# Two of three token groups go through w_in with seven block products in place of eight

## The chip, the cores and the metric

The kernel runs on one core of a Trainium2 chip. The metric is the device time of one execution in microseconds (us). Engines are named as in the profile: PE is TensorE's matmul, PEld its weight load, DVE is VectorE, ACT is ScalarE, POOL is GpSimd, and SP issues the DMAs.

## What is computed

Windowed attention over 2 batches, 8 heads and 768 positions gives 1536 tokens of width 512; two feed-forward layers follow, each with a first matrix `w_in` (512 x 2048), a pointwise function, and a second matrix `w_out` (2048 x 512).

```python
def _moe_ref(x, w_in, w_out):                 # layer 1 (L = 0 in the code)
    h = x @ w_in
    g = h * (1.0 / (1.0 + np.exp(-h)))
    return (g @ w_out).astype(np.float32)

def _moe2_ref(x, w_in, w_out):                # layer 2 (L = 1)
    h = x @ w_in
    g = np.maximum(0.01 * h, h)
    return (g @ w_out).astype(np.float32)

def reference(**kwargs):
    ...
    x = np.ascontiguousarray(attn_out.transpose(0, 2, 1, 3)).reshape(B * S, H * D)
    x = _moe_ref(x=x, **moe_kwargs)
    return _moe2_ref(x=x, **moe2_kwargs)
```

## The kernel before

The 1536 tokens are three groups of 512 (`gi` = 0, 1, 2). Each layer's 2048 inner columns are 16 chunks of 128, four to a part, so a layer has four parts. Activations lie transposed, 128 features by 512 tokens, in four tiles `x` (layer 1) or `xn` (layer 2), one for each 128 of the 512 features (`kk`). The weights come as 64-bit numbers; `load` turns a chunk into float32 with one ScalarE instruction and three VectorE instructions (L260 to L269). Every matmul operand, weight or activation, is then split into a high part (a rounded copy, index 0) and a low part (the rest, index 1): the copy is done by ScalarE or VectorE (L219, L221), the rest by a VectorE subtraction (L275). A product of two such operands takes three matmuls (`PASSES`: high by high, low by high, high by low), so a "triplet" of 512-column matmuls is the smallest piece of work on PE here.

`unit_in` makes one chunk of `h` for one group: 4 triplets into one PSUM bank `ph` (L305), then ScalarE (L313 or L315), VectorE (L320 or L322), ScalarE (L325) and VectorE (L328) make the split tile `g`. `unit_out` makes one 128-row slice of the product with `w_out` over the four chunks of a part: 4 triplets into a bank `po` (L358); ScalarE stores it in `y` in the first part (L372), VectorE adds it to `y` in the later ones (L390). After layer 1 the sums are split into `xn` (L404, L407). One group in one part thus costs 16 triplets at L305 and 16 at L358.

No order of instructions is written down by hand. `Sched` holds every piece of work as a task with a duration, a priority, its dependencies and the buffers it needs, plays them through on PE, DVE, ACT and SP with numbers of buffers from `SIZES` (8 PSUM banks `ps`, 6 tiles `g`, 5 chunks of `wi`, 6 of `wo`, 3 staging buffers `st`, ...), and writes the instructions out in the order in which they started there. Each engine then runs its own list in that order. Attention and the first part of layer 1 are interleaved in this way.

## Time and profile before

| | us |
|---|---|
| median of 3 runs | 630.77 (630.51 to 631.47) |
| the profiled execution's own time | 630.69 |
| its span, first to last instruction | 628.9 |
| PE busy in the span | 616.7 |
| DVE busy | 432.8 |
| ACT busy | 275.8 |

The profile is of one execution, so sums are made against its own 630.69 us; it lies 0.08 us under the median. Between the span and the time lie 1.79 us that the trace does not cover. In the first 143 us PE alternates between attention and the feed-forward; from there to the end it does nothing but triplets. Busy time of PE is not a measure of its work, since matmuls overlap in the records (a record lasts some 0.39 us, while one starts every 0.2267 us); its idle time is.

### The profile page before, as it was taken

The numbers are of one execution on the slowest core, as the hardware profiler recorded it, in microseconds if no ns is written. First come the engines' busy times: TensorE is split into PE (matmuls) and PEld (weight loads), VectorE is DVE, ScalarE is ACT, GpSimd is POOL, SyncE is SP. The second block draws the span as 40 slices with busy tenths as digits, with TensorE's granted clock in tenths as the row PEclk, the third lists the DMA queues.
The fourth block names the chain that finished last, engine by engine and source line by source line (L and its number), as shares of the span: only waits on it lengthen the run. The fifth ranks groups of instructions, "written<-read, shape, count | busy, mean of one in ns | idle before, by whom it ended". The sixth has DMA issues, their size and how long they took to land.

```text
span 628.9 us, 8667 instructions
## 1 busy us (share of the span) xinstructions
PE 616.7 (98%) x3191; PEld 501.1 (80%) x3191; DVE 432.8 (69%) x993; ACT 275.8 (44%) x612; POOL 2.2 (0%) x18
## 2 busy tenths in 40 slices
PE   7999999999999999999999999999999999999996
PEld 4687777778888888888888888888888888888885
DVE  6999889889653967396748881776369745954333
ACT  5898878855541244124434453444233233213210
POOL 1000000000000000000000000000000000000000
PEclk8999999999999999999999999999999999999999
DMA  8976445213230323023302330133004110200112
GB/s 189 234 181 165 114 97 141 58 40 128 68 100 1 101 69 100 1 77 91 101 1 65 103 90 11 55 113 95 6 16 132 57 64 1 68 0 18 50 68 72
DMA packets 72673, 49.40 MB, mean 79 GB/s; under 512 B 50480, under 2 KB 67120, under 8 KB 72624
## 3 DMA queue, kind: packets, MB, share of 16 engines
q1 hardware_dynamic: 72336, 48.77, 28.0%
q8 instruction: 27, 0.44, 0.3%
q14 instruction: 22, 0.18, 0.1%
q10 hardware_dynamic: 288, 0.00, 0.0%
HBM read 45.62 MB, written 3.15 MB: 78 GB/s over the span
## 4 chain that ended last, share of the span: by engine, by line
PE 92%; DVE 6%; DMA 1%; issue 0%; ACTq 0%; DVEq 0%; ACT 0%
PE po L358 42%; PE ph L305 41%; PE s L618 3%; PE pa L670 3%; PE pv L690 3%; DVE A L630 1%; PE pt L576 1%; DVE A L653 1%; DVE f L266 1%; DMA nraw<-in_n_local_dram 1%; DVE f L269 0%; DVE wi L275 0%; DVE x L699 0%; DVE f L263 0%; DVE rs L644 0%
## 5 line engine op out<-in xcount | busy, mean ns | idle before, releaser
L305 PE MATMUL ph<-x,wi 128*128 128x512 f32 (+1 forms) x624 | 146.0, 379 | 1.2 <-DVE x L699 0.4
L358 PE MATMUL po<-g,wo 128*128 128x512 f32 x576 | 139.8, 392 | 0.0
L305 PE MATMUL ph<-xn,wi 128*128 128x512 f32 x576 | 136.9, 389 | 0.0
L358 PE MATMUL po<-wo,g 128*128 128x512 f32 (+1 forms) x588 | 136.4, 385 | 0.0
L305 PEld LDWEIGHTS ph<-x,wi 128*128 128x128 f32 x624 | 110.7, 188 | 24.7 <-issue 2.2
L358 PEld LDWEIGHTS po<-wo,g 128*128 128x128 f32 x588 | 108.9, 188 | 22.0
L305 PEld LDWEIGHTS ph<-xn,wi 128*128 128x128 f32 x576 | 108.1, 188 | 22.4
L358 PEld LDWEIGHTS po<-g,wo 128*128 128x128 f32 x576 | 107.1, 188 | 23.1 <-issue 1.3
L328 DVE TENSOR_TENSOR g<-t,g 128x512 fp32r<-128x512 f32 (+1 forms) x100 | 66.6, 669 | 41.5 <-ACT g L325 40.1
L325 ACT ACTIVATE g<-t 128x512 fp32r<-128x512 f32 (+1 forms) x100 | 61.2, 616 | 66.2 <-DVE t L322 37.8
L315 ACT ACTIVATE t<-ph 128x512 f32<-128x512 f32 x48 | 28.6, 596 | 91.4 <-PE ph L305 90.5
L322 DVE TENSOR_TENSOR t<-t,ph 128x512 f32<-128x512 f32 x48 | 32.9, 686 | 37.6 <-ACT t L315 37.6
L260 ACT ACTIVATE st<-st 128x512 f32<-128x512 f32 x64 | 43.0, 672 | 31.9 <-DMA st<-in_moe_w_out_dram 23.7
L390 DVE SCALAR_TENSOR_TENSOR yp<-po,yp 128x512 f32<-128x512 f32 x48 | 33.1, 689 | 32.2 <-PE po L358 32.2
L313 ACT ACTIVATE t<-ph 128x512 f32<-128x512 f32 (+1 forms) x52 | 29.2, 563 | 53.9 <-PE ph L305 53.2
L637 ACT ACTIVATE A<-A,nm 128x256 f32<-128x256 f32 (+1 forms) x96 | 46.3, 486 | 6.0 <-DVE nm L630 5.6
L266 DVE SCALAR_TENSOR_TENSOR f<-st,f 128x512 int32<-128x512 int32 x64 | 44.0, 690 | 1.2
L269 DVE SCALAR_TENSOR_TENSOR f<-st,f 128x512 int32<-128x512 int32 x64 | 43.9, 687 | 0.5
L320 DVE SCALAR_TENSOR_TENSOR t<-t,ph 128x512 f32<-128x512 f32 (+1 forms) x52 | 33.1, 644 | 15.1 <-ACT t L313 15.0
L630 DVE CUSTOM_DVE_ANT_0 A<-s,mask 128x256 f32<-128x256 f32 (+1 forms) x96 | 35.2, 396 | 6.8 <-PE s L618 6.7
L670 PE MATMUL pa<-ident,A 128*128 128x128 f32 x176 | 26.4, 279 | 3.6 <-DVE A L653 2.4
L390 DVE SCALAR_TENSOR_TENSOR yo<-po,yp 128x512 f32<-128x512 f32 (+1 forms) x25 | 16.7, 669 | 18.9 <-PE po L358 18.9
(67 smaller groups left out, 431.4 us busy)
## 6 DMA issues: line engine op xcount, KB each, us to landing
st<-in_moe_w_in_dram SPq DMA_DIRECT2D x32, 512.0 KB, 3.7
st<-in_moe_w_out_dram SPq DMA_DIRECT2D x32, 512.0 KB, 3.5
vd<-in_v_dram SPq DMA_DIRECT2D x24, 128.0 KB, 3.0
q<-in_q_dram SPq DMA_DIRECT2D x22, 128.0 KB, 3.0
k<-in_k_dram SPq DMA_DIRECT2D x22, 128.0 KB, 3.0
out_dram<-yo SPq DMA_DIRECT2D x11, 256.0 KB, 2.0
vp<-in_v_dram SPq DMA_DIRECT2D x20, 96.0 KB, 2.7
vp<-in_v_dram SPq DMA_DIRECT2D x20, 32.0 KB, 2.4
```

Of the source, the lines that this page charges most:

```text
L260: eng.activation(hf, hf, AF.Copy, scale=2.0 ** -112)
L266: eng.scalar_tensor_tensor(fi(), lo(), 29, fi(), op0=ALU.logical_shift_right, op1=ALU.bitwise_or)
L269: eng.scalar_tensor_tensor(fi(), hi(), -(2 ** 31), fi(), op0=ALU.bitwise_and, op1=ALU.bitwise_or)
L305: eng.matmul(ph()[:, :w], wv[:, a, kk, :], xs[kk]()[:, b, cs], start=(kk == 0 and i == 0), stop=(kk == NKK - 1 and i == 2),)
L320: eng.scalar_tensor_tensor(tt, tt, 1.0, ph()[:, :w], op0=ALU.add, op1=ALU.mult)
L325: eng.activation(g()[:, 0, cs], t()[:, :w], AF.Copy)
L328: eng.tensor_tensor(g()[:, 1, cs], t()[:, :w], g()[:, 0, cs].bitcast(F32), op=ALU.subtract)
L358: eng.matmul(po()[:, :w], lhsT, rhs, start=(j == 0 and i == 0), stop=(j == FPP - 1 and i == 2))
L390: eng.scalar_tensor_tensor(dst()[:, cs], po()[:, :w], scale, y()[:, cs], op0=ALU.mult, op1=ALU.add)
L630: eng.tensor_tensor_reduce(A()[:, i, j, c0:256], s[j]()[:, i, c0:256], mask0 if c0 else mask, -QSCALE * SLOPE[2 * hp + j], 3.0e38, ALU.add ...
L637: eng.activation(a, a, AF.Exp, bias=nm()[:, x:x + 1], scale=-1.0, accum_out=su()[:, x:x + 1])
L670: eng.transpose(pa()[:, j, c, :], A()[:, i, j, c * P:(c + 1) * P], ident)
```

## The change

For groups 0 and 1, and two neighbouring chunks of `w_in` (a pair), the product is written as a product of two 2 x 2 block matrices. The weights' blocks are A11, A12 (the first chunk, lower and upper 256 of the 512 features) and A21, A22 (the second chunk); the activations' blocks are B of the lower and upper features by group 0 and group 1. A block product is two triplets (a block of weights covers two of the four 128-feature tiles). The plain product takes eight of them, 16 triplets for a pair of chunks and two groups. The change takes seven (a Strassen-Winograd scheme), 14 triplets, and adds sums:

- sums of weight blocks, S1 to S4, made by `combine` for each pair behind the weights' conversion (four half-width subtractions or additions, two splits into tiles `ws`);
- sums of activation blocks, T1 to T4, made by `sums` once in a layer (tiles `xs`; in layer 1 the split activations are first added up again);
- sums of products, made by `unit_quad`: bank a is copied to SBUF by ScalarE, five VectorE additions combine it with the banks b, c and d, and three of the four banks take a second product on top of a first one that has been read meanwhile.

`nonlin` then does what L313 to L328 did, for three of four results from SBUF and not from PSUM; in layer 2 these three need no ScalarE instruction ahead. Group 2 keeps `unit_in`, and part one of layer 1, which runs beside attention, is as before. The order in which work is offered to the planner is new: the two quads of a part, then the output of group 0, the input of group 2, the outputs of groups 1 and 2. `wi` has 4 buffers and no longer 5, `wo` 5 and no longer 6; the new tiles lie in a pool `late` that takes the place of the attention's pools, so that nothing of it can be written before the last attention unit has ended (`attn`).

The core of the diff (in layer 1, `first` is part two; in layer 2, part one):

```diff
-            w = Buf(tag, lambda: self.wp.tile([P, 2, DM], F32R, tag=tag, name=tag, bufs={"wi": 5, "wo": 6}[tag]))
...
+            w = Buf(tag, lambda: self.wp.tile([P, 2, DM], F32R, tag=tag, name=tag, bufs=SIZES[tag]))
...
+            self.f[fc % 2] = (f, t)
+            if which == "in" and self.isquad(L, fc // FPP) and fc % 2:
+                self.combine(L, fc // 2, prio)
+        def combine(self, L, pair, prio):
+            add = self.sc.add
+            (fa, _), (fb, t) = self.f[0], self.f[1]
+            res = []
+            H = DM // 2
+            for x in range(2):
+                sf = Buf("sf", lambda: self.late().tile([P, DM], F32, tag="sf", name="sf", bufs=SIZES["sf"]))
+                ws = Buf("ws", lambda: self.late().tile([P, 2, DM], F32R, tag="ws", name="ws", bufs=SIZES["ws"]))
+                if x == 0:
+                    s1 = sf
+                    ops = [(sf, 0, fb, 0, fb, 1, ALU.add), (sf, 1, sf, 0, fa, 0, ALU.subtract)]
+                else:
+                    ops = [(sf, 0, fa, 0, fb, 0, ALU.subtract), (sf, 1, fa, 1, s1, 1, ALU.subtract)]
+                for (o, oh, p, ph, q_, qh, op) in ops:
+                    def fn(eng, o=o, oh=oh, p=p, ph=ph, q_=q_, qh=qh, op=op):
+                        half = lambda b, h: b()[:, h * H:(h + 1) * H]
+                        eng.tensor_tensor(half(o, oh), half(p, ph), half(q_, qh), op=op)
+                    t = add("DVE", 0.36, fn, prio, (t, *self.attn), tuple({id(b): b for b in (o, p, q_)}.values()))
...
+                h = add(AD, (0.52, 0.36), hi, prio, (t, *self.attn), (sf, ws))
+                res.append((ws, add("DVE", 0.62, lo, prio, (h,), (sf, ws))))
+            self.w["sum", L, pair] = res
...
+        def sums(self, L):
+            add = self.sc.add
+            self.T = [[None] * 2 for _ in range(5)]
+            for kk in range(2):
+                B = {}
+                for r in range(2):
+                    for c in range(2):
+                        e = 2 * r + kk
+                        if L == 1:
+                            B[r, c] = (self.y[c, e], self.ydone[c, e])
+                            continue
+                        x = self.xs[0][c][e]
+                        f = Buf("tl", lambda: self.late().tile([P, TG], F32, tag="tl", name="tf", bufs=SIZES["tl"]))
+                        def whole(eng, x=x, f=f):
+                            eng.tensor_tensor(f(), x()[:, 0, :].bitcast(F32), x()[:, 1, :].bitcast(F32), op=ALU.add)
+                        deps = [q[2] for q in self.xdone[0][c][e]]
+                        B[r, c] = (f, add("DVE", 0.62, whole, -0.5, (*deps, *self.attn), (x, f)))
+                def make(i, p, q_, o):
...
+                    hl = [] if L == 0 or i == 3 else [self.xdone[1][{1: 0, 2: 1, 4: 0}[i]][{1: 0, 2: 2, 4: 2}[i] + kk][0][2]]
...
+                    t = add("DVE", 0.62, sub, -0.5, (pt_, qt_, ft, *hl), tuple({id(b): b for b in (f, pb, qb)}.values()))
+                    h = add("ACT", 0.52, hi, -0.5, (t, *self.attn), (f, x))
+                    self.T[i][kk] = (x, add("DVE", 0.62, lo, -0.5, (h,), (f, x)))
+                    return (f, t)
+                t1 = make(1, B[0, 1], B[0, 0], B[0, 0])
+                t3 = make(3, B[1, 1], B[0, 1], (B[0, 1][0], t1[1]))
+                t2 = make(2, B[1, 1], t1, (B[1, 1][0], t3[1]))
+                make(4, B[1, 0], t2, B[1, 0])
...
+        def unit_quad(self, n0, n1, L, pair):
...
+            j0 = (2 * pair) % FPP
+            wa, wb = self.w["in", L, 2 * pair], self.w["in", L, 2 * pair + 1]
+            (s12, t12), (s34, t34) = self.w["sum", L, pair]
+            A11, A12, A22 = (wa, 0), (wa, 1), (wb, 1)
+            S1, S2, S3, S4 = ((s12, t12), 0), ((s12, t12), 1), ((s34, t34), 0), ((s34, t34), 1)
+            X = lambda gi, r: [(self.xs[L][gi][2 * r + kk], self.xdone[L][gi][2 * r + kk][-1][2]) for kk in range(2)]
+            T = self.T
+            bank = {c: Buf("ps", lambda: self.ps.tile([P, TG], F32, tag="ps", name="pq")) for c in "abcd"}
+            def prod(c, A, Bx, first, deps=()):
+                (wt_, wd), half = A
+                def fn(kk):
+                    def mm(eng):
+                        wv = wt_().rearrange("p a (c f) -> p a c f", c=NKK)
+                        for i, (a, b) in enumerate(PASSES):
+                            eng.matmul(
+                                bank[c]()[:, :], wv[:, a, 2 * half + kk, :], Bx[kk][0]()[:, b, :],
+                                start=(first and kk == 0 and i == 0), stop=(kk == 1 and i == 2),
+                                skip_group_check=not first,
+                            )
+                    return mm
+                m = None
+                for kk in range(2):
+                    m = add("PE", 3 * 0.2267, fn(kk), self.pos, (wd, m, Bx[kk][1], *deps), (wt_, bank[c], Bx[kk][0]))
+                self.pos += 0.01
+                return m
+            tl = lambda: Buf("tl", lambda: self.late().tile([P, TG], F32, tag="tl", name="tq", bufs=SIZES["tl"]))
+            def dve(fn, deps, bufs):
+                return add("DVE", 0.62, fn, -1.0, deps, bufs)
+            p1 = prod("a", A11, X(0, 0), True)
+            p6 = prod("b", S2, T[2], True)
+            p5 = prod("c", S1, T[1], True)
+            p7 = prod("d", S3, T[3], True)
+            u2, u4, c12 = tl(), tl(), tl()
+            ba, bb, bc, bd = (bank[c] for c in "abcd")
+            e1 = add("ACT", 0.55, lambda eng: eng.activation(u2(), ba(), AF.Copy), -1.0, (p1, *self.attn), (ba, u2))
+            tu2 = dve(lambda eng: eng.tensor_tensor(u2(), u2(), bb(), op=ALU.add), (e1, p6), (u2, bb))
+            tu4 = dve(lambda eng: eng.tensor_tensor(u4(), u2(), bc(), op=ALU.add), (tu2, p5), (u2, u4, bc))
+            c22 = dve(lambda eng: eng.tensor_tensor(u4(), u4(), bd(), op=ALU.add), (tu4, p7), (u4, bd))
+            p2 = prod("a", A12, X(0, 1), False, (e1,))
+            p3 = prod("c", S4, X(1, 1), False, (tu4,))
+            p4 = prod("d", A22, T[4], False, (c22,))
+            t12_ = dve(lambda eng: eng.tensor_tensor(c12(), u2(), bc(), op=ALU.add), (tu2, p3), (u2, c12, bc))
+            t21_ = dve(lambda eng: eng.tensor_tensor(u2(), u2(), bd(), op=ALU.add), (t12_, p4), (u2, bd))
+            for (nn, j, src, dep) in ((n0, j0, ba, p2), (n1, j0 + 1, u4, c22), (n1, j0, c12, t12_), (n0, j0 + 1, u2, t21_)):
+                self.nonlin(nn, j, src, dep, src is ba, L)
...
+        def nonlin(self, n, j, src, dep, psum, L):
+            add = self.sc.add
+            g, gt = self.gbuf(n, j)
+            if L == 0 or psum:
+                t = Buf("t", lambda: self.tp.tile([P, TG], F32, tag="t", name="t"))
+                bufs = (src, t)
+                def act(eng):
+                    if L == 0:
+                        eng.activation(t(), src(), AF.Tanh, scale=0.5)
+                    else:
+                        eng.activation(t(), src(), AF.Copy, scale=0.01)
+                dep = add("ACT", 0.55, act, -1.0, (dep,), bufs)
+            else:
+                t, bufs = src, (src,)
...
+            c = add("DVE", 0.62, comb, -1.0, (dep,), bufs)
+            h = add("ACT", 0.52, hi, -1.0, (c,), (t, g))
+            gt.append(add("DVE", 0.62, lo, -1.0, (h,), (t, g)))
...
+            for n in range(NGR, N if self.quad else 0, NGR):
+                L, part, _ = self.groups[n]
+                if part == self.first[L]:
+                    self.sums(L)
+                for x in range(FPP // 2):
+                    self.unit_quad(n, n + 1, L, part * (FPP // 2) + x)
+                out(n)
+                I(n + 2, range(FPP))
+                out(n + 1)
+                out(n + 2)
+    SIZES = {"st": 3, "f": 2, "wi": 4, "wo": 5, "g": 6, "t": 3, "ps": 8, "qT": 3, "A": 2, "AT": 4, "tl": 4, "gl": 2,
+             "sf": 2, "ws": 2}
     for gi in range(NGR):
         for e in range(4):
             SIZES[f"x{gi}{e}"] = SIZES[f"y{gi}{e}"] = SIZES[f"k{e}"] = 1
+    for i in range(1, 4):
+        for kk in range(2):
+            SIZES[f"T{i}{kk}"] = 1
...
+        ea = es.enter_context(ExitStack())
+        apool = lambda name, bufs=1: ea.enter_context(tc.tile_pool(name=name, bufs=bufs))
+        ld = apool("ld", 2)
+        kp = apool("kT", 1)
+        ap_ = apool("a", 2)
+        sm = apool("sm", 4)
...
-        mo = Moe(sc, (wp, sp, cv, gp, tp, kp, xp, ps), xt, xdone,
-                 lambda L, gi, e: f"k{e}" if gi == NGR - 1 else f"y{gi}{e}")
+        mo = Moe(sc, (wp, sp, cv, gp, tp, yp, xp, ps), xt, xdone, late)
+        mo.attn = tuple(u["end"] for u in units)```

What this does to the order of the instructions is shown at three places. In the lists, a row is one instruction (x3: a triplet), output and inputs are tile names with their numbers, `pq` is a bank of a quad, `ph` and `po` are those of `unit_in` and `unit_out`.

PE, where part two of layer 1 begins. Before, the last rows of part one's output (`po`) and the first `unit_in` of part two that follow them:

```order
L358 MATMUL po_2345<-g_2152,wo_744 128x512 x3
L358 MATMUL po_2332<-g_2257,wo_931 128x512 x3
L358 MATMUL po_2345<-g_2158,wo_863 128x512 x3
L358 MATMUL po_2332<-g_2269,wo_1111 128x512 x3
L358 MATMUL po_2345<-g_2257,wo_931 128x512 x3
L305 MATMUL ph_2372<-x_312,wi_2141 128x512 x3
L358 MATMUL po_2345<-g_2269,wo_1111 128x512 x3
L305 MATMUL ph_2372<-x_400,wi_2141 128x512 x3
```

Now the first quad stands there: `pq_2345` is bank a (product 1), `pq_2364` bank b (product 6), `pq_2371` bank c (product 5, later 3 on top), `pq_2388` bank d (product 7, later 4); `xs` are sums of activations and `ws` sums of weights.

```order
L404 MATMUL pq_2364<-xs_2193,ws_2318 128x512 x3
L404 MATMUL pq_2371<-xs_2176,ws_2318 128x512 x3
L404 MATMUL pq_2364<-xs_2287,ws_2318 128x512 x3
L404 MATMUL pq_2371<-xs_2240,ws_2318 128x512 x3
L404 MATMUL pq_2388<-xs_2183,ws_2335 128x512 x3
L404 MATMUL pq_2345<-x_495,wi_2135 128x512 x3
L404 MATMUL pq_2388<-xs_2253,ws_2335 128x512 x3
L404 MATMUL pq_2345<-x_567,wi_2135 128x512 x3
L404 MATMUL pq_2371<-x_1229,ws_2335 128x512 x3
L404 MATMUL pq_2388<-xs_2206,wi_2164 128x512 x3
```

The products that need sums stand right behind part one's output, and the second products of the banks c and d (the last two rows) follow the first ones with four and two triplets between them.

VectorE, from the end of attention on. Before, the last attention result (`x_1888`) was followed by conversion of weights and by part one's results:

```order
L699 TENSOR_TENSOR x_1888<-pv_2102,x_1888 128x256
L221 CAST wi_2130<-f_2052 128x512
L275 TENSOR_TENSOR wi_2130<-f_2052,wi_2130 128x512
L320 SCALAR_TENSOR_TENSOR t_2132<-t_2132,ph_1972 128x512
L320 SCALAR_TENSOR_TENSOR t_2138<-t_2138,ph_2015 128x512
```

Now the sums of the activations begin there; of them the rows at the head (`tf` is an activation tile added up again, L366 a difference, L372 the low part of its split):

```order
L914 TENSOR_TENSOR x_1889<-pv_2097,x_1889 128x256
L353 TENSOR_TENSOR tf_2121<-x_315 128x512
L353 TENSOR_TENSOR tf_2126<-x_1046 128x512
L353 TENSOR_TENSOR tf_2133<-x_495 128x512
L507 SCALAR_TENSOR_TENSOR t_2131<-t_2131,ph_2019 128x512
L353 TENSOR_TENSOR tf_2146<-x_1229 128x512
L507 SCALAR_TENSOR_TENSOR t_2141<-t_2141,ph_2027 128x512
L515 TENSOR_TENSOR g_2148<-t_2131,g_2148 128x512
L366 TENSOR_TENSOR tf_2121<-tf_2126,tf_2121 128x512
L515 TENSOR_TENSOR g_2161<-t_2141,g_2161 128x512
L366 TENSOR_TENSOR tf_2126<-tf_2146,tf_2126 128x512
L372 TENSOR_TENSOR xs_2176<-tf_2121,xs_2176 128x512
```

The conversion of the weights of part two has moved behind the sums, as far as it was not done before the end of attention.

VectorE, in the first quad of part two of layer 1. Before, a result took two VectorE instructions there, with conversion of weights between them:

```order
L320 SCALAR_TENSOR_TENSOR t_2238<-t_2238,ph_2191 128x512
L266 SCALAR_TENSOR_TENSOR f_2245<-st_2195,f_2245 128x512
L320 SCALAR_TENSOR_TENSOR t_2255<-t_2255,ph_2212 128x512
L328 TENSOR_TENSOR g_2257<-t_2238,g_2257 128x512
L269 SCALAR_TENSOR_TENSOR f_2245<-st_2195,f_2245 128x512
L328 TENSOR_TENSOR g_2269<-t_2255,g_2269 128x512
```

Now (L429 to L435 are the additions of products, L309 the half-width sums of weights for the next pair, L316 the low part of their split):

```order
L429 TENSOR_TENSOR tq_2368<-tq_2368,pq_2364 128x512
L309 TENSOR_TENSOR sf_2392<-f_2337 128x256
L430 TENSOR_TENSOR tq_2394<-tq_2368,pq_2371 128x512
L309 TENSOR_TENSOR sf_2392<-sf_2392,f_2333 128x256
L221 CAST ws_2404<-sf_2392 128x512
L309 TENSOR_TENSOR sf_2406<-f_2333,f_2337 128x256
L431 TENSOR_TENSOR tq_2394<-tq_2394,pq_2388 128x512
L316 TENSOR_TENSOR ws_2404<-sf_2392,ws_2404 128x512
L459 SCALAR_TENSOR_TENSOR t_2415<-t_2415,pq_2345 128x512
L459 SCALAR_TENSOR_TENSOR t_2418<-t_2418,tq_2394 128x512
L309 TENSOR_TENSOR sf_2406<-f_2333,sf_2392 128x256
L435 TENSOR_TENSOR tq_2437<-tq_2368,pq_2371 128x512
```

L430 must have read bank c before product 3 may be added into it, and L431 bank d before product 4; between them in the queue stand sums of weights.

## Rows read from the trace of the kernel before

**Rows 1.** The page, part 1: busy us (share of the span) xinstructions of each engine.
```profile
PE 616.7 (98%) x3191; PEld 501.1 (80%) x3191; DVE 432.8 (69%) x993; ACT 275.8 (44%) x612; POOL 2.2 (0%) x18
```

**Rows 2.** The page, part 4: chain that ended last, by engine.
```profile
PE 92%; DVE 6%; DMA 1%; issue 0%; ACTq 0%; DVEq 0%; ACT 0%
```

**Rows 3.** Windows: us, then busy of PE, PEld, DVE, ACT, POOL; clock; DMA share; GB/s.
```profile
48.00:64.00 16.00, 14.80 (x132) 11.59 (x129) 14.97 (x54) 14.14 (x43) 0.00 (x0) 1.00 0.65 171
...
160.00:176.00 16.00, 16.00 (x72) 13.28 (x71) 10.94 (x19) 6.86 (x13) 0.00 (x0) 1.00 0.37 103
...
208.00:224.00 16.00, 16.00 (x72) 13.24 (x72) 15.39 (x27) 4.25 (x8) 0.00 (x0) 1.00 0.44 131
...
592.00:608.00 16.00, 16.00 (x72) 13.26 (x71) 6.58 (x11) 3.10 (x5) 0.00 (x0) 1.00 0.13 50
```

**Rows 4.** Chain in order of time: start us, us, what; at its end.
```profile
596.71 9.52 PE po L358 x42
607.59 4.08 PE ph L305 x18
613.03 10.37 PE po L358 x57
```

**Rows 5.** Timeline at the attention's end: start us, us, engine, line, operation, tiles.
```profile
139.82 0.39 PE L690 MATMUL pv<-AT,vd 128*64 128x128 f32 x4
...
140.14 1.65 PE L358 MATMUL po<-g,wo 128*128 128x512 f32 x6
...
140.67 0.42 DVE L699 TENSOR_TENSOR x<-pv,x 128x256 fp32r<-128x256 f32 x1 [1.18 <-ACT x L696]
```

**Rows 6.** Groups by shape: busy us, mean ns of one, idle before and its releasers.
```profile
L322 DVE TENSOR_TENSOR t<-t,ph 128x512 f32<-128x512 f32 x48 | 32.9, 686 | 37.6 <-ACT t L315 37.6
...
L263 DVE TENSOR_SCALAR f<-st 128x512 int32<-128x512 int32 x64 | 26.9, 423 | 0.9
...
L275 DVE TENSOR_TENSOR wi<-f,wi 128x512 fp32r<-128x512 f32 x32 | 22.0, 687 | 0.4
...
L221 DVE CAST wi<-f 128x512 fp32r<-128x512 f32 x22 | 9.4, 427 | 7.9 <-PE ph L305 7.4
...
L494 DVE TENSOR_TENSOR mask<-mk 128x256 f32<-128x256 f32 x1 | 0.4, 425 | 0.0
```

**Rows 7.** Groups by shape, ScalarE.
```profile
L325 ACT ACTIVATE g<-t 128x512 fp32r<-128x512 f32 x92 | 58.2, 634 | 66.2 <-DVE t L322 37.8 <-DVE t L320 28.4
...
L315 ACT ACTIVATE t<-ph 128x512 f32<-128x512 f32 x48 | 28.6, 596 | 91.4 <-PE ph L305 90.5
```

**Rows 8.** Timeline of VectorE in two stretches in which it never sits idle.
```profile
271.90 0.68 DVE L320 SCALAR_TENSOR_TENSOR t<-t,ph 128x512 f32<-128x512 f32 x1
272.50 0.68 DVE L275 TENSOR_TENSOR wi<-f,wi 128x512 fp32r<-128x512 f32 x1
...
283.07 0.69 DVE L266 SCALAR_TENSOR_TENSOR f<-st,f 128x512 int32<-128x512 int32 x1
283.80 0.69 DVE L269 SCALAR_TENSOR_TENSOR f<-st,f 128x512 int32<-128x512 int32 x1
...
289.35 0.69 DVE L328 TENSOR_TENSOR g<-t,g 128x512 fp32r<-128x512 f32 x1
...
464.61 0.69 DVE L275 TENSOR_TENSOR wi<-f,wi 128x512 fp32r<-128x512 f32 x1
...
483.80 0.68 DVE L322 TENSOR_TENSOR t<-t,ph 128x512 f32<-128x512 f32 x1
```

**Rows 9.** Timeline of one chunk's result in a quiet stretch, and a matmul's record.
```profile
257.68 0.39 PE L358 MATMUL po<-g,wo 128*128 128x512 f32 x1
...
262.93 0.60 ACT L313 ACTIVATE t<-ph 128x512 f32<-128x512 f32 x1 [11.90 <-PE ph L305]
263.56 0.69 DVE L320 SCALAR_TENSOR_TENSOR t<-t,ph 128x512 f32<-128x512 f32 x1 [3.40 <-ACT t L313]
264.28 0.63 ACT L325 ACTIVATE g<-t 128x512 fp32r<-128x512 f32 x1 [0.76 <-DVE t L320]
```

More of the change, by code (lines that the diff above doesn't have):

```diff
@@ new lines, in isquad, with ypool, gbuf @@
+        def isquad(self, L, part):
+            return self.late is not None and self.first[L] <= part
+        def ypool(self, gi):
+            return self.late() if self.late and gi == NGR - 1 else self.yp
+        def gbuf(self, n, j):
+            if (n, j) not in self.g:
+                if self.isquad(*self.groups[n][:2]) and j == FPP - 1:
+                    b = Buf("gl", lambda: self.late().tile([P, 2, TG], F32R, tag="gl", name="g", bufs=SIZES["gl"]))
+                else:
+                    b = Buf("g", lambda: self.gp.tile([P, 2, TG], F32R, tag="g", name="g"))
+                self.g[n, j] = (b, [])
+            return self.g[n, j]
@@ L295, in unit_in @@
             t = Buf("t", lambda: self.tp.tile([P, TG], F32, tag="t", name="t"))
[L296 to L298 removed]
+            g, gt = self.gbuf(n, j)
             xs = self.xs[L][gi]
@@ L374, in evac @@
                         eng.tensor_scalar(y(), po(), scale, None, op0=ALU.mult)
-                self.ydone[gi, e] = add("ACT", 0.55, evac, -1.0, (m,), (po, y))
+                self.ydone[gi, e] = add("ACT", 0.55, evac, -1.0, (m, *(self.attn if gi == NGR - 1 else ())), (po, y))
                 return
             y = self.y[gi, e]
-            if not last:
+            if not last or (L == 0 and self.quad and gi < 2):
                 dst = y
@@ L392, in acc @@
                 )
-            a = add("DVE", 0.07 + 0.55 * r, acc, -1.0, (m, self.ydone[gi, e]), (po, y, dst))
+            a = add("DVE", 0.07 + 0.55 * r, acc, -1.0, (m, self.ydone[gi, e]), (po, y, dst) if dst is not y else (po, y))
             self.ydone[gi, e] = a
-            if not last:
+            if not last or (L == 0 and self.quad and gi == 1 and e < 2):
                 return
@@ L515 @@
         add("DVE", 0.6, lambda eng: flags(), 20.0, (mtask,), at=20.0)
-        zero = const.tile([P, TG], mybir.dt.bfloat16, name="zero")
+        zero = kp.tile([P, TG], mybir.dt.bfloat16, name="zero")
         nc.vector.memset(zero, 0.0)
```

85 lines of the change are left out of this document (59 added, 26 removed).

## The prediction

> **What bounds the kernel now.** I read the page first, then the chain of waits, then the windows. The page gives PE 98% of the span [rows 1], and the chain that ends last runs through PE for 92% of it [rows 2]. A busy share alone proves little, so the windows decide: until about 64 us PE has gaps (14.80 of 16 us busy at 48 to 64 us), and from there to the end it has none, while VectorE is anywhere between 6.6 and 15.4 of 16 us [rows 3]. The chain in order of time shows the rate: 42 matmuls of 512 columns in 9.52 us, 0.2267 us each, without a gap up to 623.40 us [rows 4]; a triplet is 0.680 us. The granted clock is 1.00, the upper of its two levels (2.4 GHz), in all these windows [rows 3]. So a triplet that is taken away after the attention gives back 0.680 us, as long as PE still never waits. The whole question is whether VectorE and ScalarE can deliver the sums in time.
>
> **What is removed.** A pair of chunks costs 14 triplets and not 16, for groups 0 and 1 together. There are two pairs to a part and seven changed parts (three of layer 1, four of layer 2): 14 x 2 = 28 triplets, 84 matmuls. The order of the changed kernel has 28 triplet rows less on PE, so it does what it says. At 0.2267 us that is 19.04 us, all of it on the path [rows 2, 4]. If nothing waits: 630.69 - 19.04 = 611.65 us. A changed part has 276 matmuls, 62.6 us of PE; before it had 288, 65.3 us.
>
> **What is added, and its prices.** Per pair VectorE gets four half-width sums of weights and two full-width low parts, and five full-width additions of products; per layer it gets 16 full-width instructions for the T sums (24 in layer 1). No such row exists before; the nearest are subtractions of SBUF tiles (687 ns) and a maximum of an SBUF tile with a bank (686 ns) for the full width, one 128x256 sum (425 ns) for the half width [rows 6]. The reading of SBUF or PSUM makes no difference between these rows, so I take 0.69 and 0.425 us as durations, with casts and shifts at 0.43 [rows 6]. Together: 14 x (4 x 0.425 + 7 x 0.69) + 40 x 0.69 = 119 us more on VectorE, 433 to about 552 of then some 612 us.
>
> Durations overstate what a full queue costs. In a stretch where VectorE never idles, an instruction that doesn't need the one before it starts 0.60 us after it (271.90 to 272.50), one that does 0.73 us after it (283.07 to 283.80). Over two whole stretches, 29 instructions (22 long, 7 short; 18.1 us by duration) took 17.45 us, and 33 (24 long, 9 short; 20.3 us) took 19.19 us [rows 8]: 0.96 and 0.94 of the durations. I take 0.94, the lower one, because conversions, in which each instruction needs the one before, are a smaller part of the new order; the ends are 0.60 and 0.36 us for each long and short one, and the bare durations.
>
> The Trainium skill, page "VectorE: DVE Perf Modes", section "The DRAIN you can't avoid", says that the next instruction doesn't start until the pipeline is empty. By that rule the bare durations would hold; the 0.60 us above speak against it for independent instructions, 0.73 us for it where one needs the other. What the time would be by the rule is rival B.
>
> With these, counted from the changed order between the first addition of one part's first quad and that of the next, VectorE has: layer 1 part two 82 long and 27 short, 64.0 us (58.9 to 68.1); part three 60.4 (55.7 to 64.3); part four 57.7; layer 2 part one 79 and 33, 64.4 us (59.3 to 68.5); then 55.3, 54.1 and 32.5. PE has 62.6 us in each. So two parts are full to the brim and the others have room.
>
> ScalarE gets a copy of bank a per pair (0.60 us), the high parts of the T sums (0.63 us), and those of the weight sums that VectorE doesn't take; it loses three copies per pair in layer 2 (0.60 us) [rows 7]. At 276 us busy of 629 [rows 1] it has room for that: nothing on the path.
>
> **Where PE could wait, place by place.**
>
> *Entry.* PE's order is the same as before until shortly ahead of the attention's end; up to there ScalarE and VectorE only lack the conversion of a fifth `wi` chunk. The last attention product ends at 140.2 us, VectorE's last instruction for it at 141.1 [rows 5]; in the new order one triplet less stands ahead of it, so PE is 0.7 us earlier. From there PE has 41 triplets, 27.9 us, to the first product that needs sums: 140.2 - 0.7 + 27.9 = 167.4 us. VectorE has 35 long and 4 short to that point, 24.3 us (22.4 to 25.8): 165.4 (163.5 to 166.9). It fits: 0. The tiles of the new pool also wait for the attention's reads and loads, which are over by then: 0.
>
> *First part with quads.* VectorE keeps a backlog: the conversion of part two's `w_out` stands behind the sums. To the last of its four chunks it has 87 long and 17 short from 141.1 us on, 63.2 us (58.3 to 67.3), so 204.3 (199.4 to 208.4). PE needs that chunk 91 triplets after attention's end, at 201.4 us. The wait is 2.9 us (0 to 7.0). Behind that point VectorE only follows the outputs of PE and wins the room back.
>
> *First part of layer 2.* The T sums of layer 2 stand in the last output of layer 1, the first weights' sums for the second pair and `w_out` behind them. From the first addition to the fourth `w_out` chunk VectorE has 48 long and 10 short, 35.1 us (32.4 to 37.4); PE needs it 50 triplets after product 6, 34.0 us, less 0.2 us for the last matmul's tail (a record of 0.39 us against 0.2267 [rows 9]). The wait is 1.3 us (0 to 3.6).
>
> *Bank handover in each quad.* Product 3 waits for the addition that reads bank c, product 4 for that which reads bank d. After product 6, four triplets and more (2.7 us) cover a tail of 0.16 and two additions with hops of 0.03 us (262.93 + 0.60 to 263.56 [rows 9]), 1.6 us. After product 7 two triplets (1.36 us) cover a tail, a hop and one addition, 0.9 us: 0.46 us to spare, less than one long instruction in front. ScalarE, which copies bank a, waits on PE alone there. I take 0.1 us for each of 14 quads, 1.4 us (0 to 4.2, at 0.3).
>
> *Buffers.* With four `wi` and five `wo` the next weights come later, but the first chunk of the next part is converted 34 triplets, 23 us, before its use in the order, and DMA runs at 0.13 to 0.44 of its time there [rows 3]: 0. If that cover were gone, a load and its conversion would show, some 6 us a part; nothing points to it.
>
> Sum: 611.65 + 2.9 + 1.3 + 1.4 = 617.25 us; low end 611.65, high end 611.65 + 7.0 + 3.6 + 4.2 = 626.5. The profiled run is 0.08 us under the median, which changes nothing. I say 617.3.
>
> **Rivals.**
>
> *A, PE never waits.* For it: before, PE had no gap even where VectorE was 15.39 of 16 us busy [rows 3], and by the 0.60 us pitch every place above comes out at zero. Against: two parts with more than 62.6 us of work at the measured ratio. 611.7 us.
>
> *B, VectorE sets the pace of three parts.* With bare durations layer 1 part two loses 7.0 us, part three 64.3 - 62.6 = 1.7, layer 2 part one 5.9; with the handovers 16.0 us: 627.7 us. Against it stand both ratios below one [rows 8].
>
> *C, slower than before.* The handover becomes a wait in every quad, because VectorE comes to it with a queue in front: the second part's cover is 0.46 us, and a further long instruction ahead of the addition costs 0.60. The gain is gone when each of the 14 quads waits 19.04 / 14 = 1.36 us, that is from three more long instructions on ((3 x 0.60 - 0.46) = 1.34). With four it is 14 x 1.94 = 27.2 us: 638.8 us. For it: VectorE runs in its order and waits itself for ScalarE (37.6 us idle ahead of L322 alone [rows 6]), and what stands behind the waiting instruction waits with it. Against: in the order only half-width sums and a cast stand between the additions, and five of the seven parts have room.
>
> **How the numbers follow.** The forecast's mechanism, waits of 1.5 to 13 us in the two full parts and at handovers (613 to 625 us), gets 0.74, A 0.10, B 0.07, C 0.06, and 0.03 is left for sums that happen to end within 0.2% of before, which is about what a measurement here can tell from no change (1.3 us). Range 611.5 to 626.5 us: it takes in A and the upper bounds of the three waits and leaves out B, C and the rest, 0.16. Faster by over 0.2%: 0.74 + 0.10 + 0.07 = 0.91; same 0.03; slower 0.06.
>
> **What would show it.** PE should have 3107 instructions and idle about 5 us more than 12.2 us; its waits should name VectorE: `wo` or `ws` low parts between about 185 and 205 us and again in the first 35 us of layer 2, and next to nothing in layer 2 parts two to four, where the triplets should run at 0.680 us. VectorE should be near 550 us busy. The changed parts should take 62.6 us but for the two named. I am wrong if PE waits in every quad for L430 or L431 (C), if windows of the two full parts show PE without a gap (A), if part three of layer 1 is stretched too (B), or if the clock falls below 1.00 behind a wait.

## The result and the profile after

The changed kernel takes 612.77 us (611.97 to 613.20) against 631.12 us, a ratio of 0.9708 (0.9691 to 0.9724): 18.4 us less. A second set (run e1 below) gives 0.9705 (0.9692 to 0.9718), 19.1 us less. The 84 triplet matmuls that are gone are worth 19.04 us. The forecast of 617.3 us had 5.6 us of waits in it that did not come: it is rival A, PE never waits, that happened. The time lies in the range only because the range's low end was set to take in A; the mechanism that was given 0.74 did not show.

The profiled execution took 613.08 us (span 611.3). Its page, busy time and chain by engine, against [rows 1, 2]:

```profile
PE 598.4 (98%) x3107; PEld 485.9 (79%) x3107; DVE 519.6 (85%) x1172; ACT 300.4 (49%) x657; POOL 2.2 (0%) x18
...
PE 93%; DVE 5%; DMA 1%; issue 0%; SPq 0%; ACT 0%; ACTq 0%; DVEq 0%
```

PE is idle for 12.9 us (611.3 - 598.4), before for 12.2. VectorE has 87 us more and PE has not noticed. The windows, against [rows 3] (busy of PE, PEld, DVE, ACT, POOL; clock; DMA share; GB/s); the last one is the first part of layer 2:

```profile
160.00:176.00 16.00, 16.00 (x73) 13.24 (x72) 15.71 (x32) 7.77 (x14) 0.00 (x0) 1.00 0.22 67
176.00:192.00 16.00, 16.00 (x72) 13.28 (x71) 15.85 (x28) 10.08 (x18) 0.00 (x0) 1.00 0.11 33
192.00:208.00 16.00, 16.00 (x73) 13.24 (x72) 15.70 (x28) 8.17 (x14) 0.00 (x0) 1.00 0.44 132
354.60:416.50 61.90, 61.90 (x274) 51.26 (x273) 60.03 (x111) 31.10 (x53) 0.00 (x0) 1.00 0.32 97
```

VectorE is full in the stretches that the prediction named (15.7 to 15.9 of 16 us; 60.03 of 61.90), and in others too (15.97 of 16 us from 480 to 496 us, in layer 2's part three). PE shows no gap in the named ones, the sign that the prediction had given for A. The list of what PE's weight loads waited for from 150 us on has one line (us in total, times, longest):

```profile
PEld pq L404 <- DVE tq L431: 0.3, 1, 0.3
```

It is the handover in the first quad of layer 2's part two. PE starts its triplet there 0.07 us late (424.73 us, where 423.98 + 0.68 = 424.66) and the one behind it another 0.11 us:

```profile
423.99 0.68 DVE L431 TENSOR_TENSOR tq<-tq,pq 128x512 f32<-128x512 f32 x1
```

```profile
423.98 0.84 PE L404 MATMUL pq<-xn,ws 128*128 128x512 f32 x3
424.73 0.96 PE L404 MATMUL pq<-xs,wi 128*128 128x512 f32 x3
425.52 0.86 PE L404 MATMUL pq<-xn,ws 128*128 128x512 f32 x3
```

How close it is elsewhere, the timelines tell. Layer 1's part two: the low parts (L278) of its four `w_out` chunks on VectorE, and L431, the addition that frees bank d for product 4, in the second quad:

```profile
141.20 1.89 DVE L353 TENSOR_TENSOR tf<-x 128x512 f32<-128x512 f32 x3
...
185.48 0.69 DVE L431 TENSOR_TENSOR tq<-tq,pq 128x512 f32<-128x512 f32 x1
...
188.57 0.69 DVE L278 TENSOR_TENSOR wo<-f,wo 128x512 fp32r<-128x512 f32 x1
...
194.92 0.68 DVE L278 TENSOR_TENSOR wo<-f,wo 128x512 fp32r<-128x512 f32 x1
...
198.64 0.68 DVE L278 TENSOR_TENSOR wo<-f,wo 128x512 fp32r<-128x512 f32 x1
...
201.05 0.69 DVE L278 TENSOR_TENSOR wo<-f,wo 128x512 fp32r<-128x512 f32 x1
```

and PE there:

```profile
186.64 0.84 PE L404 MATMUL pq<-xs,wi 128*128 128x512 f32 x3
...
189.36 2.88 PE L545 MATMUL po<-g,wo 128*128 128x512 f32 x12
...
196.16 2.88 PE L545 MATMUL po<-g,wo 128*128 128x512 f32 x12
...
199.56 5.60 PE L545 MATMUL po<-g,wo 128*128 128x512 f32 x24
```

Each group of four output triplets needs one more chunk, so the chunks are wanted at 189.36, 196.16, 199.56 and 202.28 us (199.56 + 4 x 0.68); they are ready at 189.26, 195.60, 199.32 and 201.74. The smallest margin is 0.10 us. L431 ends at 186.17, and product 4 wants its bank at 186.64: 0.47 us. In the first part of layer 2 the fourth chunk is ready at 390.61 + 0.68 = 391.29 us and wanted at 385.90 + 8 x 0.68 = 391.34:

```profile
385.90 8.32 PE L545 MATMUL po<-wo,g 128*128 128x512 f32 x36
...
390.61 0.68 DVE L278 TENSOR_TENSOR wo<-f,wo 128x512 fp32r<-128x512 f32 x1
```

### The profile page after: what moved, and what is told of

It reads as the page before. It is cut to its first block, busy times and chain, and to the rows that moved or that the text cites. A ratio compares the mean times of both kernels' runs of the same rounds, so it can differ in the third digit from the quotient of the medians.

```text
span 611.3 us, 8732 instructions
## 1 busy us (share of the span) xinstructions
PE 598.4 (98%) x3107; PEld 485.9 (79%) x3107; DVE 519.6 (85%) x1172; ACT 300.4 (49%) x657; POOL 2.2 (0%) x18
## 4 chain that ended last, share of the span: by engine, by line
PE 93%; DVE 5%; DMA 1%; issue 0%; SPq 0%; ACT 0%; ACTq 0%; DVEq 0%
PE po L545 43%; PE pq L404 22%; PE ph L492 17%; PE s L833 3%; PE pa L885 3%; PE pv L905 3%; PE pt L791 2%; DVE A L845 1%; DVE A L868 1%; DMA nraw<-in_n_local_dram 1%; DVE f L269 0%; DMA k<-in_k_dram 0%; DVE wi L278 0%; DVE f L266 0%; DVE f L272 0%
## 5 line engine op out<-in xcount | busy, mean ns | idle before, releaser
L545 PE MATMUL po<-g,wo 128*128 128x512 f32 x576 | 139.0, 391 | 0.0
L545 PE MATMUL po<-wo,g 128*128 128x512 f32 (+1 forms) x588 | 135.6, 385 | 0.0
L545 PEld LDWEIGHTS po<-wo,g 128*128 128x128 f32 x588 | 108.9, 188 | 22.0
L545 PEld LDWEIGHTS po<-g,wo 128*128 128x128 f32 x576 | 107.2, 188 | 22.9 <-issue 1.0
L492 PE MATMUL ph<-x,wi 128*128 128x512 f32 (+1 forms) x336 | 78.0, 369 | 1.1 <-ACT x L911 0.4
L492 PEld LDWEIGHTS ph<-x,wi 128*128 128x128 f32 x336 | 56.6, 188 | 13.5 <-issue 2.2
L404 PE MATMUL pq<-xs,ws 128*128 128x512 f32 x252 | 63.8, 389 | 0.0
L263 ACT ACTIVATE st<-st 128x512 f32<-128x512 f32 x64 | 42.9, 670 | 27.4 <-DMA st<-in_moe_w_out_dram 19.4
L404 PEld LDWEIGHTS pq<-xs,ws 128*128 128x128 f32 x252 | 47.3, 188 | 9.8
L492 PE MATMUL ph<-xn,wi 128*128 128x512 f32 x192 | 47.1, 389 | 0.0
L269 DVE SCALAR_TENSOR_TENSOR f<-st,f 128x512 int32<-128x512 int32 x64 | 43.4, 684 | 0.4
L492 PEld LDWEIGHTS ph<-xn,wi 128*128 128x128 f32 x192 | 36.0, 188 | 7.5
L512 ACT ACTIVATE g<-t 128x512 fp32r<-128x512 f32 (+1 forms) x44 | 25.6, 591 | 18.4 <-DVE t L509 10.1
L502 ACT ACTIVATE t<-ph 128x512 f32<-128x512 f32 x16 | 9.5, 593 | 43.1 <-PE ph L492 33.2
L515 DVE TENSOR_TENSOR g<-t,g 128x512 fp32r<-128x512 f32 (+1 forms) x44 | 27.6, 637 | 1.2 <-ACT g L512 0.7
L833 PE MATMUL s<-kT,qT 64*128 64x256 f32 (+1 forms) x192 | 27.6, 396 | 0.6 <-DVE kT L803 0.5
```

The source lines that it names most:

```text
L263: eng.activation(hf, hf, AF.Copy, scale=2.0 ** -112)
L269: eng.scalar_tensor_tensor(fi(), lo(), 29, fi(), op0=ALU.logical_shift_right, op1=ALU.bitwise_or)
L404: eng.matmul(bank[c]()[:, :], wv[:, a, 2 * half + kk, :], Bx[kk][0]()[:, b, :], start=(first and kk == 0 and i == 0), stop=(kk == 1 and i ...
L492: eng.matmul(ph()[:, :w], wv[:, a, kk, :], xs[kk]()[:, b, cs], start=(kk == 0 and i == 0), stop=(kk == NKK - 1 and i == 2),)
L515: eng.tensor_tensor(g()[:, 1, cs], t()[:, :w], g()[:, 0, cs].bitcast(F32), op=ALU.subtract)
L545: eng.matmul(po()[:, :w], lhsT, rhs, start=(j == 0 and i == 0), stop=(j == FPP - 1 and i == 2))
```

## The experiments

Two theories stand against each other. The forecast: VectorE takes 0.94 of its durations and is late in two parts. Rival A, made sharper by the trace of after: VectorE advances by 0.60 us per long instruction, and with that arrives just in time everywhere. To compare runs whatever their first 160 us did, the table gives the stretch from the first quad product (the timeline) to the end of PE's last row in the chain in order of time, all from the one profiled execution of each run. After and its repetition e1 start it at 166.24 and 165.14 us, and their chains' last rows of PE are these: 438.80 us both times.

```profile
585.51 19.53 PE po L545 x96
```

```profile
584.41 19.53 PE po L545 x96
```

In e11 and e12 the chain follows PE to its very last matmul, 0.34 us further (x102 in place of x96); that is taken off in the table:

```profile
594.76 20.57 PE po L546 x102
```

| run | median, us | ratio to before (interval) | stretch, us | against after |
|---|---|---|---|---|
| e1, after again | 612.1 | 0.9705 (0.9692 to 0.9718) | 438.80 | 0 |
| e2, before, small pools | 631.07 | 1.0001 (0.9992 to 1.0010) | | |
| e3, layer 2 only | 620.7 | 0.9835 (0.9820 to 0.9850) | | |
| e4, eight products' triplets | 631.34 | 1.0000 (0.9991 to 1.0010) | 457.66 | +18.86 |
| e5, one more at handover | 614.93 | 0.9748 (0.9733 to 0.9763) | 441.40 | +2.60 |
| e6, three more at handover | 630.5 | 0.9991 (0.9981 to 1.0000) | 457.00 | +18.20 |
| e7, four more in layer 1's part two | 614.46 | 0.9737 (0.9724 to 0.9751) | 440.75 | +1.95 |
| e9, group 2 three of four | 598.39 | 0.9477 (0.9461 to 0.9493) | 424.91 | -13.89 |
| e10, group 2 two of four | 590.6 | 0.9351 (0.9335 to 0.9366) | 417.66 | -21.14 |
| e11, planned too cheap | 623.02 | 0.9861 (0.9844 to 0.9879) | 448.80 | +10.00 |
| e12, planned too dear | 617.43 | 0.9773 (0.9755 to 0.9790) | 445.86 | +7.06 |

**Is the gain the matmul count and nothing else?** e1 repeats after. e2 changes before:

```diff
-            w = Buf(tag, lambda: self.wp.tile([P, 2, DM], F32R, tag=tag, name=tag, bufs={"wi": 5, "wo": 6}[tag]))
+            w = Buf(tag, lambda: self.wp.tile([P, 2, DM], F32R, tag=tag, name=tag, bufs={"wi": 4, "wo": 5}[tag]))
...
```

e3 lets the quads begin with layer 2 (the loops' bounds follow):

```diff
-            self.first = (1, 0)
+            self.first = (4, 0)
```

e4 makes the first triplet of product 1 three times:

```diff
+                        n = 3 if c == "a" and first and kk == 0 else 1
-                        for i, (a, b) in enumerate(PASSES):
+                        for i, (a, b) in enumerate(PASSES * n):
...
```

> The changed kernel as it is, beside the kernel before. The profiled run of after ended its PE work 0.7 us later than 19.04 us less would give, and all of that was there by the end of the attention, after a stretch from 8 to 20 us in which the granted clock was lower than in the profiled run of before (0.88, 0.50, 0.77 against 1.00, 0.57, 1.00 in windows of 4 us). If this is a chance of the single execution, the two kernels' mean clocks overlap and the gain is 18.3 to 19.0 us, ratio 0.970 to 0.971. If the smaller pool of weight buffers delays the attention stage, after stays at a mean clock of 0.992 to 0.995 below that of before in nearly all runs, and the gain stays at 18.0 to 18.4 us.

> The kernel before with 4 buffers for w_in chunks and 5 for w_out chunks, as in the changed kernel, and with nothing else changed; all products are the plain ones. The prediction put the smaller pools at nothing, because a chunk of the next part is converted some 23 us before its use: 630.8 to 631.3 us. If the smaller pools cost something on their own (in the attention stage, or because a chunk comes too late), it is slower by 0.5 to 1 us for the first and by up to 6 us a part for the second.

> Seven products in the four parts of layer 2 only; layer 1 is as before (with the smaller pools). 16 x 3 = 48 matmuls fewer than before, at 0.2267 us: 10.88 us. If PE's count alone sets the time (PE never waits), 631.1 - 10.9 = 620.2 us, ratio 0.983. By the forecast a wait of 1.3 us in the first part of layer 2 and 8 x 0.1 us at the bank handovers come on top: 622.3 us, ratio 0.986.

> The changed kernel with its sums, buffers and order, but each quad computes the first triplet of its first product three times, so that 16 triplets stand on PE as in the plain product: 84 matmuls more than after. If the gain is nothing but the 84 matmuls at 0.2267 us, the time is that of before, 631.1 us with 0.7 us either way (ratio 0.999 to 1.001), though VectorE still carries all the added instructions. If the new order, the pools or the added VectorE work cost or bring something of their own that the smaller count hides, it is off by that: by the forecast's waits up to 5 us slower than before if they stay, though 2.7 us more of PE in each part should cover most of them.

All four went as PE's count says. e3 gains 10.5 us of 10.88, where the forecast had 8.8. e4 is back at the time of before with all of the added VectorE work in it, so that work, the new order and the pools are free as long as they are in time. e2 shows that the smaller pools cost nothing in the kernel before. The 0.7 us that the first set lacked need no cost of the change: 19.04 us less would be a ratio of 0.970, inside the intervals of both sets, and the second set has 19.1 us. A time also follows the mean clock of its execution (after: 613.44 us at 0.992, 611.90 at 0.995; before: 632.22 at 0.993, 630.30 at 1.000), which differs by how long the clock stays low between 8 and 20 us. The nine executions of after all lie at 0.992 to 0.995, but e5 and e7, which run the same order up to there, reach 0.999.

**What does VectorE really take?** e8 puts four times ten instructions in front of accumulations in layer 2's part four.

```diff
+                if (L, part, gi) == (1, NPART - 1, 1):
+                    self.again(eng, [self.y[2, x] for x in range((1, 2, 4, 4)[e])], 10, TG if e < 3 else 256)
```

> The changed kernel with four groups of ten more VectorE instructions in layer 2's part four, ahead of the four accumulations of group 1's output: ten long ones each needing the one before, ten long ones each needing the last but one, ten long ones each needing the fourth before, ten of 256 columns each needing the fourth before. It measures the pitch by itself. From the traces: 0.73 us start to start for the first, 0.60 for the third; the second is what decides whether orders with one instruction between two dependent ones go at 0.60 (then the sum by the lower ends, 58 to 59 us for the two full parts, is the right one) or near 0.67 (then the ratio of 0.94 is); half width: 0.33 to 0.43 us. By durations alone all long ones would take 0.69. The output is right, PE may wait here, and the time is of no account.

Timeline of VectorE in e8, the four groups (start us, us for all ten):

```profile
586.40 7.22 DVE L246 TENSOR_TENSOR yp<-yp 128x512 f32<-128x512 f32 x10
...
594.74 6.10 DVE L246 TENSOR_TENSOR yp<-yp 128x512 f32<-128x512 f32 x10
...
601.37 6.09 DVE L246 TENSOR_TENSOR yp<-yp 128x512 f32<-128x512 f32 x10
...
607.99 3.42 DVE L246 TENSOR_TENSOR yp<-yp 128x256 f32<-128x256 f32 x10
```

With the last one's duration taken off, nine steps of (7.22 - 0.69) / 9 = 0.73 us when each needs the one before, 0.60 us when each needs the last but one, 0.60 us for the fourth before, and (3.42 - 0.41) / 9 = 0.33 us for half the width. One instruction in between is enough. That is the order of a kernel that interleaves several chains. The 0.94 of [rows 8] came from stretches in which conversions, each step needing the one before, took a larger part: in the full timelines 14 of 29 and 14 of 33 steps there are longer than these pitches, in after from 141.20 to 201.05 us 14 of 103, and the others keep to 0.60 and 0.34 us.

The Trainium skill, page "Vector Engine (DVE) Microarchitecture Reference", section "5.2 Measured stream behaviour on trn2 (trn3 not measured)", gives 1.0417 ns per column and about 75 ns per instruction after overlap, from integer streams of 1024 columns and more. As an estimate for 512 and 256 columns that is 0.61 and 0.34 us; the 0.60 and 0.33 us here agree, the 0.73 us does not. The Trainium skill's section "The DRAIN you can't avoid" (page "VectorE: DVE Perf Modes"), weighed in the prediction, limits its own rule, which the prediction left out: "A next op that is not held starts earlier". The 0.60 us agrees with that sentence; the bare duration of 0.69 us is neither pitch.

**How much room is there?** e5 and e6 (shown) put one and three long instructions ahead of L431, e7 puts four ahead of the second `w_out` chunk of layer 1's part two.

```diff
+        def again(self, eng, tiles, n, w=TG):
+            for i in range(n if self.quad else 0):
+                t = tiles[i % len(tiles)]()[:, :w]
+                eng.tensor_tensor(t, t, t, op=ALU.max)
...
-            c22 = dve(lambda eng: eng.tensor_tensor(u4(), u4(), bd(), op=ALU.add), (tu4, p7), (u4, bd))
+            c22 = dve(lambda eng: (self.again(eng, (u2, u4), 3), eng.tensor_tensor(u4(), u4(), bd(), op=ALU.add)), (tu4, p7), (u4, bd))
```

> The changed kernel with one more long VectorE instruction (a maximum of a 128x512 tile with itself, which changes no value) in each of the 14 quads, directly ahead of the addition that frees bank d (L431). In the trace of after that addition ends 0.47 us ahead of product 4's first triplet in both quads of layer 1's part two. Cover arithmetic: 0.60 - 0.47 = 0.13 us in each quad, 1.8 us, and in layer 1's part two and the first part of layer 2, where VectorE has next to nothing to spare, up to 1.2 us more each (two such instructions): 612.3 + 1.8 to 4.2 = 614 to 616.5 us. If VectorE mostly comes to the handover with time to spare: 612.3 us, and no wait of PE names L431. By rival C as written one more instruction already costs 0.14 us per quad, three cost 1.34.

> As the run before, with three more long instructions in each quad (1.8 us). Cover arithmetic and rival C alike: 1.8 - 0.47 = 1.33 us of wait in each of 14 quads, 18.7 us, so the gain of the change is gone: 612.3 + 18.7 = 631 us, with VectorE's added load of 3.6 us a part lying inside these waits of 2.7 us a part but for up to 1 us in each of the two full parts (631 to 633 us). If the handover has more cover than counted, because PE has other triplets to put between the products: under 622 us.

> The changed kernel with four more long VectorE instructions (maximum of a tile with itself) once, in layer 1's part two, at the start of the conversion of its second w_out chunk, before the low parts of the four chunks that PE then waits for. In the trace of after the low parts end at 189.26, 195.60, 199.32 and 201.74 us and PE's first triplets that need them start at 189.36, 196.16, 199.56 and 202.28 us, so 0.10 us is the smallest margin. At a pitch of 0.60 the addition is 2.4 us; if VectorE is at the brim there, PE waits about 2.3 us and the time is 612.3 + 2.3 = 614.6 us. If VectorE has room to catch up (it merely runs just in time because it follows PE), 612.3 to 613 us.

Waits of PE's weight loads from 150 us on, first in e5, then in e6 (L436 there is L431 of after):

```profile
PEld pq L409 <- DVE tq L436: 2.7, 6, 0.9
PEld po L550 <- DVE wo L283: 0.5, 2, 0.3
```

```profile
PEld pq L409 <- DVE tq L436: 17.2, 14, 2.1
...
PEld po L550 <- DVE wo L283: 1.0, 2, 0.8
```

One more costs 2.60 us, by waits at L431 in six of the 14 quads and at the chunks. The cover that the expectations took from layer 1's part two does not hold everywhere: read in the same way from the timelines of after, L431 ends 0.47 us ahead of product 4 in eight of the 14 quads, 1.0 to 1.7 us in five, and in the one shown above it is at its limit. Three more cost 18.20 us, and the gain is gone. That is 1.30 us per quad where 1.33 was counted, but as an average: from one quad's product 4 to the next PE's delay against after grows by 0.4 to 2.6 us, since covers differ and chunks and results come late too. So rival C's point of decision was right and its price right on average; it did not happen because L431 comes in time in 13 of the 14 quads. e7 lost 1.95 of its 2.40 us, and the place was mainly the handover ahead of the chunks: 1.76 us, with 0.2 us at the first chunk. In all it is the 2.40 less the handover's margin of 0.47. PE's timeline there:

```profile
185.18 0.84 PE L500 MATMUL ph<-x,wi 128*128 128x512 f32 x3
187.62 0.96 PE L412 MATMUL pq<-xs,wi 128*128 128x512 f32 x3 [1.59 <-DVE tq L439]
```

**When does VectorE become the bound?** e9 (shown) and e10 (with 2 for 1) take PE work away by leaving part of group 2's input product out, and leave VectorE's:

```diff
-                    for i, (a, b) in enumerate(PASSES):
+                    k0 = 1 if self.isquad(L, part) else 0
+                    for i, (a, b) in enumerate(PASSES if kk >= k0 else ()):
...
```

> The changed kernel, but group 2's input product in the seven parts with quads leaves out the first of its four 128-feature tiles (one triplet per chunk, 4 per part, 28 in all). PE has 19.04 us less, 59.9 us a part in place of 62.6; VectorE and ScalarE keep all their work and the order stands. It asks how near VectorE is to being the bound. If VectorE has far more room than counted: 612.3 - 19.0 = 593.3 us. If its pitch is 0.60 us with margins of 0.1 to 0.5 us ahead of the w_out chunks of layer 1's part two, that part and the first of layer 2 can give back next to nothing of their 2.7 us each, the other five do: 593.3 + 4 to 5 = 597.5 us. By the forecast's ratio of 0.94 three parts would be at their limit (64.0, 60.4, 64.4 us of VectorE against 59.9), with 4.1 + 0.5 + 4.5 us of waits beyond the handovers: 603 us.

> As the run before, with two of group 2's four 128-feature tiles left out (56 triplets, 38.1 us less than after; 57.1 us of PE a part). VectorE far away: 574.2 us. Pitch of 0.60: layer 1's part two (58.9 us and more of VectorE) and layer 2's part one (59.3 and more) stay near 60 to 61 us, layer 1's part three (55.7 and more) loses up to 1 us, the handovers as before: 574.2 + 8 to 10 = 583 us. By the ratio of 0.94: 64.0 + 60.4 + 57.7 + 64.4 against 57.1 each, 6.9 + 3.3 + 0.6 + 7.3 = 18.1 us of waits: 592 us.

e9 gave back 13.89 of 19.04 us, within 1 us of what the pitch of 0.60 had it give (598.39 us; 597.5 was expected, 603 by the ratio). The distance from one part's first quad product to the next shrank by 2.7 us in layer 1's part three (63.92 to 61.24) and in layer 2's part two (62.76 to 60.03), and grew by 0.1 us in layer 2's part one (61.90 to 62.04): that part has nothing left to give. Layer 1's part two still gave 1.5 us (61.20 to 59.69), where next to nothing was expected. e10 missed: 590.6 us, not 583, and it lies nearer to the 592 us by the ratio of 0.94. It is not that ratio, though: in its part one of layer 2, nine in ten of VectorE's steps behind a long instruction take 0.60 us, as in after. That part took 65.09 us, longer than with more PE work; VectorE was busy there for 15.48 of the first 16.40 us and for all of the next 16.00, which fits that it had to make up for what PE had run ahead in the parts before. PE's longest waits there are for a `w_out` chunk (2.2 us) and for sums of activations on ScalarE (1.3 us). A comparison of sums per part is too kind here; why e10 lost just this much was not shown.

**Why is everything just in time?** e11 and e12 change only the price at which the planner counts a long VectorE instruction of layer 2, to 0.50 (shown) and 0.75 us:

```diff
+    VP = (0.62, 0.5)
...
-            t = add("DVE", 0.62, op_c, prio, (t,), (st, f))
+            t = add("DVE", VP[L], op_c, prio, (t,), (st, f))
```

> The changed kernel, planned with 0.50 us for a long VectorE instruction of layer 2 in place of 0.62 (layer 1 keeps 0.62; only the order changes, no work). It asks why PE never waited though VectorE was busy for 60.0 of 61.9 us in layer 2's part one. If PE is covered because the planner wrote its order with a price (0.62) just above the measured pitch (0.60), so that PE's list has group 2's triplets wherever the sums are late, an order planned with 0.50 puts products and outputs too early: in layer 2's part one some 48 long instructions at 0.10 too little, up to 4.8 us of waits, and more handovers at the limit: 614 to 618 us. If the order doesn't matter, because VectorE simply has less to do than PE: 612.3 us.

> The same with 0.75 us in place of 0.62 for layer 2. If a price above the measured pitch is safe for PE, 612.3 us as before, though the plan itself then has more VectorE work in layer 2's part one than PE work and puts PE triplets of later units ahead. If a wrong price in either direction costs, because buffers then fill in another order than planned: 613 to 618 us.

The same instructions in another order cost 10.00 and 7.06 us (5 us in e12's median; its profiled execution is the slowest of four). The longest waits of PE from 150 us on, in e11 and in e12:

```profile
PEld pq L405 <- DVE tq L432: 3.7, 4, 1.6
PEld pq L405 <- DVE tq L431: 2.6, 6, 0.9
PEld po L546 <- DVE wo L279: 2.2, 2, 1.8
```

```profile
PEld po L546 <- DVE wo L279: 3.4, 1, 3.4
```

Planned too cheap, the handovers and chunks come too late for PE's list, and it costs nearly twice the most that was expected. Planned too dear is no safe side either: the planner then puts group 2's input ahead of the second quad, and PE comes to one late chunk with nothing to put before it. This fits the reading that the margins of 0.05 to 0.5 us come from an order made with 0.62 us, close to the 0.60 that the chip takes. It is not shown: no order planned at 0.60, or at another price near 0.62, was run, so it may be that any other order costs.

## Why the prediction was right and wrong

- *What is removed*: right. 84 x 0.2267 = 19.04 us; 19.07 us in the second set, and in e4 the same triplets cost 18.86.
- *Prices*: the step that failed. The prediction had 0.60 us from a row and 0.94 of durations from two stretches [rows 8], and took the second. Its reason, fewer conversions in the new order, was right in direction, but the step that followed, the lower of two measured ratios, was too small. From 141.20 to 201.74 us the 104 instructions took 60.5 us, not 63.2: 0.90 of their durations. At the pitches of e8 they take 87 x 0.60 + 17 x 0.33 = 57.8. The other 2.7 us is in the 14 steps longer than that: three of them hold 0.74 us in which VectorE idles for ScalarE, and only some of the others stand between dependent instructions.
- *Entry*: right. VectorE had the first sums ready at 164.71 us (L316, 164.02 + 0.69), PE wanted them at 168.28; no wait.
- *First part with quads*, 2.9 us: it was 0. The chunk was wanted at 202.28 us and ready at 201.74, so the term was off by 3.4 us: 2.7 of the pitch, 0.8 because VectorE began 0.8 us behind PE's count and not 1.6. The part was right, the chunk was not: the tightest is the first, at 0.10 us, the fourth has 0.54. e7 shows how little room the part has, 0.45 us of the 2.40 added.
- *First part of layer 2*, 1.3 us: it was 0, at a margin of 0.05 us for the fourth chunk. The 58 instructions took 33.5 us (357.81 to 391.29), not 35.1.
- *Handover*, 1.4 us: it was next to 0, 0.2 us in one quad. The cover was right for eight quads (0.47 us, 0.46 counted), in five it was larger, and what lies beyond it costs on average what was counted (e6); the allowance of 0.1 for a queue that no row showed was too much.
- *Buffers* and *ScalarE* at nothing: right (e2; no transfer among PE's waits).
- *VectorE near 550 us busy*: 519.6. The 119 us added were summed by durations, while busy time in the records counts overlapping instructions once: by durations, after has 594 us and before 485, not 432.8. And the planner left VectorE fewer high parts of weights: 42 casts of `wi` and `wo` before, 21 in after and 9 of `ws`.
- *Chances*: A had 0.10, too little, with its reason written beside it ("by the 0.60 us pitch every place above comes out at zero").

## What to carry to other kernels

Count a full VectorE by the start-to-start pitch that fits its dependencies, and not by durations or by a ratio from a stretch of other work; then compare ready and wanted times place by place, since a part can be full to 0.05 us without a wait. Where a planner writes the order, its price per instruction is part of the result: 0.12 or 0.13 us off cost a quarter to a half of this gain. Before adding instructions ahead of a handover, look at its cover, and in every place where it occurs: here 0.47 us in eight of 14 quads, and three instructions more took the whole gain.

## What the runs showed of the hardware

A wait of PE can cost more than itself. In e12 PE stood still from 385.3 to 388.48 us, as its timeline shows:

```profile
385.10 0.39 PE L546 MATMUL po<-wo,g 128*128 128x512 f32 x1
388.48 34.13 PE L546 MATMUL po<-wo,g 128*128 128x512 f32 x137 [2.99 <-DVE wo L279]
```

The granted clock then fell to the lower of its two levels (1.2 GHz) for some 7 us (the windows at 0.94, 0.50 and 0.70 below), and was back at the upper one (2.4 GHz) by 396 us. The windows of e12, columns as in the windows of after:

```profile
380.00:384.00 4.00, 4.00 (x19) 3.02 (x18) 4.00 (x8) 0.36 (x1) 0.00 (x0) 1.00 0.00 0
384.00:388.00 4.00, 1.49 (x7) 0.91 (x5) 3.93 (x7) 1.91 (x3) 0.00 (x0) 0.94 0.41 131
388.00:392.00 4.00, 3.52 (x8) 2.84 (x9) 3.85 (x7) 0.65 (x2) 0.00 (x0) 0.50 0.16 30
392.00:396.00 4.00, 4.00 (x14) 3.17 (x13) 1.73 (x4) 1.15 (x2) 0.00 (x0) 0.70 0.70 232
396.00:400.00 4.00, 4.00 (x19) 3.29 (x18) 2.76 (x5) 1.71 (x3) 0.00 (x0) 1.00 0.34 91
```

The row at 388.48 us has 137 matmuls in 34.13 us; at 0.2267 us each they take 136 x 0.2267 + 0.39 = 31.2. The low clock thus cost 2.9 us on top of the wait. This execution was 2.3 us above its median (619.74 against 617.43), which fits: its mean clock was 0.990, that of the others 0.992 to 0.996. In e10 two waits close together (1.25 and 0.40 us idle) brought 0.62 in the window behind them, while a single one of 2.23 us there and the waits of e6, up to 1.70 us of idle PE each, left it at 1.00.
